# Attention, gated MLP and top-2 experts on one core: one addition becomes a tensor_reduce, and the conversion of the first weights is spread in another way

## The chip, the cores and the metric

The kernel runs on one NeuronCore of a Trainium2 chip. A NeuronCore has five engines that run side by side, each through its own list of instructions in order, and wait for each other by semaphores: TensorE (PE in the profile; the loading of weights into it is PEld), VectorE (DVE), ScalarE (ACT), GpSimd (POOL) and SyncE (SP), which here issues most of the DMAs. The metric is the device time of one execution in microseconds (us); lower is better.

## The reference

Three layers follow each other. All inputs come from the host in one launch.

```
# 1. attention: B=4, H=8 heads, S=576, D=64; heads 0-3 see the last 32 positions,
#    heads 4-7 every 32nd position before them
scores = where(mask, q @ k.T / sqrt(D), -1e9)
attn   = exp(scores - max(scores))
attn   = attn / (sum(attn) + 1e-9)
x      = attn @ v                         # 2304 tokens x 512
# 2. MLP: 512 -> 2048 -> 512
h = x @ w_in ;  x = (h * sigmoid(1.702 * h)) @ w_out
# 3. eight experts, two per token, chosen by noisy logits: 512 -> 1024 -> 512
out[t] = sum over the 2 experts of weight * (relu(x @ w1[e]) @ w2[e])
```

The weights w_in and w_out of the MLP arrive as 64-bit floats.

## The kernel before, in words

**Numbers in two halves.** TensorE multiplies rounded 32-bit values (fp32r). To keep the precision, a matrix is held as a high part (the rounded value) and a low part (what is left), and each product is three matmuls: high times high, high times low, low times high. L460, L461 and L462 are these three of the first MLP product, L486 to L488 those of the second. L462 is the first of the three that reads the low part of a weight.

**MLP weights.** The hidden 2048 columns are 16 slices of 128 (`fc`). Slice fc has two pieces of 512 columns: piece (fc, 0) belongs to w_in and is read by `m1_l1` (L451), piece (fc, 1) to w_out and is read by `m1_l2` (L478). A piece goes through four stations:

- `w_raw` (L355) loads its 64-bit words by DMA on SP's queue; there are four such buffers;
- `w_bits` (L416) makes 32-bit floats of them with three operations of 128x512 on DVE: L421, L424, L428. In the prologue the intermediate value stands in PSUM (`pb`), afterwards in SBUF (`cv`);
- `w_split` (L388) makes the high part on ACT (L392) and the low part on POOL (L393). It takes what was converted before the last call of `w_split`, so a piece is split one call later than the next one at hand;
- then `w_raw` asks for the piece two slices on.

`w_step` (L402) hands out one piece per call; the code takes one of the three operations at each `next(conv)`.

**Attention.** It is cut into groups (one batch, a pair of heads, a part of the positions). A group goes through scores on PE (L222 or L237), masking and minimum on DVE (L185), exponents and their sums on ACT (L190), `normalize` (L193), transposes on PE (L250 or L255), a copy on ACT, the product with v on PE (L267 or L277), and the high and low part of x (ACT L206, DVE L209). In `normalize` DVE adds 1e-9 to the sums (L194) and takes the reciprocal (L196); for the first 28 groups POOL multiplies by it (L198), afterwards DVE does (L202). The small numbers of a group stand in a tile `st` with four buffers.

**Order of the work.** Everything around the change is in an order written by hand: engines PE, ACT, DVE and POOL run their instructions in the order of the code.

- The prologue (loop at L901, steps k = 0, 1, ...) works through the first 14 groups of attention, so that the MLP can begin on the first tokens. In the steps named by `CONVAT` a piece of the weights is converted too. `warm` matmuls (L888) on a tile of ones keep PE busy.
- Then come the slices (loop at L957, number i). Slices 0 to 7 work on tokens 0 to 383 with fc = i; slices 8 to 23 work on tokens 384 to 767 with fc = i - 8, and so on. In slices 0 to 7 DVE, ACT and POOL also do two groups of attention each. A slice runs `m1_l1` of itself, some attention, `m1_l2` of the slice before, more attention. Each slice converts one piece in its first half (L968, `conv = w_step()`); the line `conv = w_step() if i < HALFC and not i % 2 or ...` adds a second one in its second half for i = 0, 2, 4, 6. `w_split` is called twice in a slice, in the middle and at the end.
- In the second half of a slice with a second piece, DVE does L421, L424, L194, L428 and L196 in this order, since `normalize` takes one operation of the piece between its own two.

## Time and profile before

| what | value |
|---|---|
| three runs | 971.8, 973.03 and 973.61 us, median 973.03 |
| the profiled execution | 971.91 us |
| its span in the trace | 970.1 us |
| PE busy | 951.4 us (98%) |
| DVE busy | 531.3 us (55%) |
| ACT busy | 387.0 us (40%) |
| POOL busy | 218.0 us (22%) |
| first matmul of the MLP (L460) | 35.25 us after the span's start |
| granted TensorE clock | mean 0.998 |

Busy time counts matmuls with a modelled end, so a busy PE is not a PE at its peak. The chain of work that ended last is PE for 82%, DVE for 8%. DVE's busy tenths are 7 to 9 of 10 in the first 120 us and 3 to 6 later. A duration in the trace contains the time that an instruction waited after it had begun, so the same operation on the same tile can show 0.15 and 1.26 us.

### The profile page before, as it was taken

The page shows a single profiled execution, that of the slowest core. Times are in us where ns is not written, and L with a number is a line of the kernel's source. Part 1 is how long each engine was busy: PE and PEld are TensorE (multiplying, and loading weights), DVE is VectorE, ACT ScalarE, POOL GpSimd, SP SyncE. Part 2 cuts the span into 40 slices and gives each one's busy share as a digit, 9 for nine tenths or more (in the row PEclk, how much of TensorE's full clock was granted, in tenths as well). Part 3 has the DMA queues.
Part 4 walks back from the last instruction along what each step waited for, and adds up shares of the span by engine and source line. Part 5 has one row for each costly group of instructions (what it writes and reads, how often), then busy time and mean ns, then how long its engine had stood idle before and what let it go on. Part 6 is the DMA issues. An engine that isn't in the chain of part 4 may idle for free.

```text
span 970.1 us, 15925 instructions
## 1 busy us (share of the span) xinstructions
PE 951.4 (98%) x5706; PEld 839.3 (87%) x5706; DVE 531.3 (55%) x1518; ACT 387.0 (40%) x1031; POOL 218.0 (22%) x206
## 2 busy tenths in 40 slices
PE   7999999999999999999999999999999999999996
PEld 4778899898888889899898998888988889898994
DVE  7899865467646745632666343545546363635511
ACT  6865533344444444223254242333424242433411
POOL 3566231020200100020230522050412305050303
PEclk9999999999999999999999999999999999999999
DMA  9754521052324236301064158275674938576503
GB/s 337 254 193 164 173 70 66 1 118 61 57 88 113 68 70 216 149 1 66 3 194 142 31 140 217 87 176 172 140 221 109 237 113 204 151 170 177 107 1 53
DMA packets 83793, 123.93 MB, mean 128 GB/s; under 512 B 13488, under 2 KB 42800, under 8 KB 83696
## 3 DMA queue, kind: packets, MB, share of 16 engines
q1 hardware_dynamic: 73888, 102.92, 34.5%
q0 software_dynamic: 9824, 19.98, 11.0%
q8 instruction: 45, 0.74, 0.3%
q14 instruction: 36, 0.29, 0.1%
HBM read 93.33 MB, written 29.68 MB: 127 GB/s over the span
## 4 chain that ended last, share of the span: by engine, by line
PE 82%; DVE 8%; issue 5%; ACT 2%; DMA 1%; POOL 1%; SPq 0%; POOLq 0%; DVEq 0%; ACTq 0%
PE pb L827 6%; PE pb L826 6%; PE pb L828 6%; PE pb L486 6%; PE pb L845 6%; PE pb L460 6%; PE pb L847 6%; PE pb L846 6%; PE pb L461 6%; PE pb L462 6%; PE pb L488 6%; PE pb L487 6%; DVE area L428 1%; PE pb L237 1%; PE pb L222 1%
## 5 line engine op out<-in xcount | busy, mean ns | idle before, releaser
L831 DVE SCALAR_TENSOR_TENSOR ht<-pb,ht 128x352 fp32r<-128x352 f32 (+2 forms) x126 | 59.2, 472 | 170.8 <-ACT ht L830 170.8
L460 PE MATMUL pb<-xt,w 128*128 128x384 f32 x384 | 131.8, 343 | 0.0
L461 PE MATMUL pb<-xt,w 128*128 128x384 f32 x384 | 129.6, 338 | 0.0
L462 PE MATMUL pb<-xt,w 128*128 128x384 f32 x384 | 129.5, 337 | 0.0
L830 ACT ACTIVATE ht<-pb 128x352 fp32r<-128x352 f32 (+2 forms) x126 | 53.1, 424 | 182.0 <-PE pb L828 181.2
L845 PE MATMUL pb<-w,ht 128*128 128x512 f32 (+1 forms) x315 | 124.0, 394 | 0.0
L846 PE MATMUL pb<-w,ht 128*128 128x512 f32 (+1 forms) x315 | 123.3, 391 | 0.0
L847 PE MATMUL pb<-w,ht 128*128 128x512 f32 (+1 forms) x315 | 123.2, 391 | 0.0
L863 POOL DMA_INDIRECT out<-y,el x40 | 63.1, 1578 | 266.5 <-ACT y L862 237.8
L486 PE MATMUL pb<-w,g 128*128 128x512 f32 x288 | 118.2, 410 | 0.3 <-ACT g L474 0.2
L488 PE MATMUL pb<-w,g 128*128 128x512 f32 x288 | 113.2, 393 | 0.0
L487 PE MATMUL pb<-w,g 128*128 128x512 f32 x288 | 112.5, 391 | 0.0
L469 DVE SCALAR_TENSOR_TENSOR th<-th,pb 128x384 f32<-128x384 f32 x96 | 52.7, 549 | 107.0 <-ACT th L465 107.0
L655 POOL DMA_INDIRECT lst<-pay,si x36 | 35.7, 992 | 326.9 <-DVE si L652 285.3
L680 DVE TENSOR_TENSOR w<-raw,w 128x512 fp32r<-128x512 f32 x128 | 85.3, 688 | 28.5 <-ACT w L679 27.5
L465 ACT ACTIVATE th<-pb 128x384 f32<-128x384 f32 x96 | 46.9, 489 | 128.4 <-PE pb L462 118.0
L679 ACT CAST w<-raw 128x512 fp32r<-128x512 f32 x128 | 76.0, 619 | 35.9 <-DMA raw<-wm 33.0
L826 PE MATMUL pb<-xt,w 128*128 128x352 f32 (+1 forms) x256 | 84.0, 328 | 0.0
L828 PE MATMUL pb<-xt,w 128*128 128x352 f32 (+1 forms) x256 | 83.5, 326 | 0.0
L827 PE MATMUL pb<-xt,w 128*128 128x352 f32 (+1 forms) x256 | 83.4, 326 | 0.0
L460 PEld LDWEIGHTS pb<-xt,w 128*128 128x128 f32 x384 | 72.1, 188 | 4.8 <-issue 1.0
L461 PEld LDWEIGHTS pb<-xt,w 128*128 128x128 f32 x384 | 72.1, 188 | 3.8 <-DVE xt L209 0.2
(193 smaller groups left out, 1925.1 us busy)
## 6 DMA issues: line engine op xcount, KB each, us to landing
raw<-wm SPq DMA_DIRECT2D x136, 256.0 KB, 3.0
area<-wm SPq DMA_DIRECT2D x28, 512.0 KB, 4.3
xs<-g SPq DMA_DIRECT2D x24, 256.0 KB, 3.7
out<-zero SPq DMA_DIRECT2D x7, 768.0 KB, 7.3
att<-attS SPq DMA_DIRECT2D x20, 253.0 KB, 4.5
qk<-attL SPq DMA_DIRECT2D x16, 304.0 KB, 4.3
tr<-xs SPq DMA_DIRECT2D x24, 176.0 KB, 3.4
att<-attL SPq DMA_DIRECT2D x8, 496.0 KB, 8.3
```

What stands on the lines that cost most here:

```text
L460: nc.tensor.matmul(ps, w[0][:, a], X[c][:, 0, kc, :], start=(n == 0), stop=False)
L461: nc.tensor.matmul(ps, w[0][:, a], X[c][:, 1, kc, :], start=False, stop=False)
L462: nc.tensor.matmul(ps, w[1][:, a], X[c][:, 0, kc, :], start=False, stop=(n == 3))
L486: nc.tensor.matmul(o, g[:, 0, a], w[0], start=((c, fc) in FIRST), stop=False)
L487: nc.tensor.matmul(o, g[:, 0, a], w[1], start=False, stop=False)
L488: m = nc.tensor.matmul(o, g[:, 1, a], w[0], start=False, stop=((c, fc) in LAST))
L826: nc.tensor.matmul(ps, w[:, 0, a], x[:, 0, kc, :], start=(kc == 0), stop=False)
L827: nc.tensor.matmul(ps, w[:, 0, a], x[:, 1, kc, :], start=False, stop=False)
L828: nc.tensor.matmul(ps, w[:, 1, a], x[:, 0, kc, :], start=False, stop=(kc == 3))
L845: nc.tensor.matmul(o, hi, w[:, 0, 512:], start=(fc == 0), stop=False)
L846: nc.tensor.matmul(o, hi, w[:, 1, 512:], start=False, stop=False)
L847: m = nc.tensor.matmul(o, lo, w[:, 0, 512:], start=False, stop=(fc == NF2 - 1))
```

## The change

The 1e-9 is no longer added in place. One tile `stats` takes the place of the four `st`; its row 2 holds 1e-9 for good, and a `tensor_reduce` sums rows 1 (the sums) and 2 into row 3, from which the reciprocal goes to row 4. In the prologue four pieces are converted and not six, in steps 5, 7, 9 and 11 and not in 4, 6, 7, 9, 11 and 13. Slices 1, 2, 4, 5, 9 and 10 convert two pieces, and not slices 0, 2, 4 and 6. The load of the sixth group of attention moves ahead of the first piece of weights.

```
-CONVAT = (4, 6, 7, 9, 11, 13)
+TWICE = (1, 2, 4, 5, 9, 10)
+CONVAT = (5, 7, 9, 11)
...
+    stats = const.tile([128, 4, 5, 4], F32, name="stats")
...
         def normalize(p, st, q, nt, w, pool, conv):
-            nc.vector.tensor_scalar(st[:q, 1, :nt], st[:q, 1, :nt], 1e-9, None, op0=OP.add)
+            nc.vector.tensor_reduce(st[:q, 3, :nt], st[:q, 1:3, :nt].rearrange("p a t -> p t a"),
+                                    axis=AX.X, op=OP.add)
             next(conv, None)
-            nc.vector.reciprocal(st[:q, 2, :nt], st[:q, 1, :nt])
+            nc.vector.reciprocal(st[:q, 4, :nt], st[:q, 3, :nt])
...
-            st = tmp.tile([128, 3, 4], F32, tag="st", name="st", bufs=4)
...
-                    self.sm[i] = g_scores(self.gs[i], self.ld[i], banks[i % len(banks)])
+                    self.sm[i] = g_scores(self.gs[i], self.ld[i], banks[i % len(banks)], stats[:, i % 4])
...
+        nc.vector.memset(stats[:, :, 2], 1e-9)
...
-        att.load(5)
+        att.load(6)
         w_raw(0, 0)
         att.load(2)
         w_raw(0, 1)
-        att.load(1)
         w_raw(1, 0)
         w_raw(1, 1)
...
-            conv = w_step() if i < HALFC and not i % 2 or i >= SMALLS else iter(())
+            conv = w_step() if i in TWICE or i >= SMALLS else iter(())
```

The line numbers of the changed kernel are 2 or 3 higher: L194 becomes L196, L196 becomes L199, L198 becomes L201, L393 becomes L395, L421, L424 and L428 become L423, L426 and L430, L460 to L462 become L462 to L464, L469 becomes L471, L476 becomes L478.

**DVE in the prologue, before**, from the first operation of piece (0, 1) to that of piece (1, 0) (`area_130` and `area_135` are their raw buffers):

```order
L421 TENSOR_SCALAR pb7_70<-area_130 128x512
L185 ISA att_128,st_240<-pb0_63,cs_74 126x126
L185 ISA st_240 126x1
L185 ISA att_128,st_240<-pb0_63,cs_74 126x126
L185 ISA st_240 126x1
L424 SCALAR_TENSOR_TENSOR pb7_70<-area_130,pb7_70 128x512
L428 SCALAR_TENSOR_TENSOR area_130<-area_130,pb7_70 128x512
L194 TENSOR_SCALAR st_214<-st_214 126x2
L196 RECIPROCAL st_214<-st_214 126x2
L209 TENSOR_TENSOR xt_101<-pb5_68,xt_101 128x7x18
L421 TENSOR_SCALAR pb7_70<-area_135 128x512
```

The same step with the change, up to the first operation of piece (0, 1), now `area_134`:

```order
L187 ISA att_130,stats_78<-pb0_63,cs_74 126x126
L187 ISA stats_78 126x1
L187 ISA att_130,stats_78<-pb0_63,cs_74 126x126
L187 ISA stats_78 126x1
L196 TENSOR_REDUCE stats_78<-stats_78 126x2
L199 RECIPROCAL stats_78<-stats_78 126x2
L212 TENSOR_TENSOR xt_102<-pb5_68,xt_102 128x7x18
L423 TENSOR_SCALAR pb7_70<-area_134 128x512
```

Two steps of the prologue (4 and 13) lose a conversion, and the one of step 6 moves to step 5.

**POOL in slices 3 to 5, before** (`w1_5_626` and `w1_6_713` are the slots of the weights of fc = 5 and 6; L476 is once in a slice, L198 twice):

```order
L198 TENSOR_TENSOR att_532<-att_532,st_780 72x2x72
L476 TENSOR_TENSOR g_806<-th_805,g_806 128x384
L393 TENSOR_TENSOR w1_5_626<-area_627,w1_5_626 128x512
L198 TENSOR_TENSOR att_620<-att_620,st_822 126x2x126
L393 TENSOR_TENSOR w1_5_626<-area_675,w1_5_626 128x512
L198 TENSOR_TENSOR att_622<-att_622,st_856 126x2x126
L476 TENSOR_TENSOR g_880<-th_879,g_880 128x384
L198 TENSOR_TENSOR att_707<-att_707,st_896 126x2x126
L393 TENSOR_TENSOR w1_6_713<-area_714,w1_6_713 128x512
```

The same engine with the change, from slice 4 to slice 6 (`w1_5_715`, `w1_6_793`, `w1_7_896` are the slots of fc = 5, 6, 7):

```order
L201 TENSOR_TENSOR att_584<-att_584,stats_78 126x2x126
L478 TENSOR_TENSOR g_840<-th_839,g_840 128x384
L201 TENSOR_TENSOR att_667<-att_667,stats_78 126x2x126
L395 TENSOR_TENSOR w1_5_715<-area_716,w1_5_715 128x512
L201 TENSOR_TENSOR att_669<-att_669,stats_78 126x2x126
L478 TENSOR_TENSOR g_914<-th_913,g_914 128x384
L395 TENSOR_TENSOR w1_5_715<-area_751,w1_5_715 128x512
L201 TENSOR_TENSOR att_747<-att_747,stats_78 72x2x72
L395 TENSOR_TENSOR w1_6_793<-area_794,w1_6_793 128x512
L478 TENSOR_TENSOR g_986<-th_985,g_986 128x384
L395 TENSOR_TENSOR w1_6_793<-area_823,w1_6_793 128x512
L395 TENSOR_TENSOR w1_7_896<-area_897,w1_7_896 128x512
```

Before, the place behind the second L198 of slice 4 is that of piece (6, 0); now it is that of piece (5, 0). The split of piece (fc, 0) for fc = 5, 6, 7 has moved from one slice earlier to the end of the slice just ahead of the one that reads it.

**PE at the start of slice 5, before**:

```order
L277 MATMUL pb7_70<-att_620 64x126
L255 MATMUL pb6_69<-cs_74,att_622 126x126 [waits Pool_49]
L255 MATMUL pb6_69<-cs_74,att_622 126x126
L237 MATMUL pb5_68<-att_709 126x126 [waits DMAHW2_49,DVE_49]
L237 MATMUL pb5_68<-att_709 126x126
L460 MATMUL pb1_64<-xt_101,w1_5_626 128x384
L461 MATMUL pb1_64<-xt_101,w1_5_626 128x384
L462 MATMUL pb1_64<-xt_101,w1_5_626 128x384
```

With the change:

```order
L279 MATMUL pb7_70<-att_582 64x126
L257 MATMUL pb6_69<-cs_74,att_584 126x126 [waits Pool_49]
L257 MATMUL pb6_69<-cs_74,att_584 126x126
L239 MATMUL pb5_68<-att_669 126x126 [waits DMAHW7_49,DVE_49]
L239 MATMUL pb5_68<-att_669 126x126
L462 MATMUL pb1_64<-xt_102,w1_5_715 128x384 [waits Activation_49]
L463 MATMUL pb1_64<-xt_102,w1_5_715 128x384
L464 MATMUL pb1_64<-xt_102,w1_5_715 128x384 [waits Pool_49]
```

The first matmul of the slice now waits for ACT (the high part) and the third for POOL (the low part). The same two waits stand at the start of slices 3, 4, 6 and 7 with the change, and at none of them before.

## Rows read from the trace of the kernel before

**Rows 1.** Busy us (and instructions) by stretch: PE, PEld, DVE, ACT, POOL, clock, DMA share.
```profile
0.00:35.20 35.20, 28.82 (x217) 18.72 (x218) 27.10 (x143) 25.65 (x107) 16.13 (x25) 1.00 0.94 350
35.20:86.20 51.00, 48.98 (x340) 39.73 (x339) 45.87 (x131) 31.85 (x110) 31.78 (x31) 1.00 0.49 164
```

**Rows 2.** Waits of PE from 35.2 to 90 us: total us, times, longest.
```profile
PE pb L277 <- DVE xt L209: 1.0, 2, 0.5
PE pb L267 <- DVE xt L209: 0.5, 1, 0.5
PE pb L277 <- DVE st L185: 0.4, 1, 0.4
```

**Rows 3.** DVE in the prologue, in order of time: start us, duration us, instruction.
```profile
10.16 0.69 DVE L421 TENSOR_SCALAR pb<-area 128x512 int32<-128x512 int32 x1 [0.69 <-DMA area<-wm]
...
20.54 0.70 DVE L421 TENSOR_SCALAR pb<-area 128x512 int32<-128x512 int32 x1
...
24.78 0.69 DVE L421 TENSOR_SCALAR pb<-area 128x512 int32<-128x512 int32 x1
...
31.77 0.26 DVE L185 CUSTOM_DVE_ANT_0 att<-pb,cs 128x96 f32<-128x96 f32 x1
...
34.34 0.25 DVE L185 CUSTOM_DVE_ANT_0 att<-pb,cs 128x96 f32<-128x96 f32 x1
```

**Rows 4.** PE in slices 3 to 7, the third and last L462 of each.
```profile
57.88 0.34 PE L462 MATMUL pb<-xt,w 128*128 128x384 f32 x1
...
63.33 0.34 PE L462 MATMUL pb<-xt,w 128*128 128x384 f32 x1
...
64.91 0.33 PE L462 MATMUL pb<-xt,w 128*128 128x384 f32 x1
...
69.88 0.34 PE L462 MATMUL pb<-xt,w 128*128 128x384 f32 x1
...
71.47 0.34 PE L462 MATMUL pb<-xt,w 128*128 128x384 f32 x1
...
76.44 0.34 PE L462 MATMUL pb<-xt,w 128*128 128x384 f32 x1
...
78.03 0.34 PE L462 MATMUL pb<-xt,w 128*128 128x384 f32 x1
...
82.45 0.34 PE L462 MATMUL pb<-xt,w 128*128 128x384 f32 x1
```

**Rows 5.** DVE in slices 3 to 6.
```profile
60.54 0.53 DVE L469 SCALAR_TENSOR_TENSOR th<-th,pb 128x384 f32<-128x384 f32 x1
...
63.30 1.26 DVE L194 TENSOR_SCALAR st<-st 126x2 f32<-126x2 f32 x1
...
67.09 0.53 DVE L469 SCALAR_TENSOR_TENSOR th<-th,pb 128x384 f32<-128x384 f32 x1
...
69.92 0.43 DVE L421 TENSOR_SCALAR cv<-area 128x512 int32<-128x512 int32 x1
...
71.72 0.16 DVE L196 RECIPROCAL st<-st 126x2 f32<-126x2 f32 x1
...
78.98 0.56 DVE L469 SCALAR_TENSOR_TENSOR th<-th,pb 128x384 f32<-128x384 f32 x1
```

**Rows 6.** POOL in slices 3 and 4.
```profile
62.79 1.74 POOL L393 TENSOR_TENSOR w<-area,w 128x512 fp32r<-128x512 f32 x1
...
72.59 1.47 POOL L393 TENSOR_TENSOR w<-area,w 128x512 fp32r<-128x512 f32 x1
```

**Rows 7.** ACT at the end of slice 6.
```profile
82.55 0.62 ACT L392 CAST w<-area 128x512 fp32r<-128x512 f32 x1
```

**Rows 8.** All of L194: duration in ns, minimum, median, maximum.
```profile
L194 DVE TENSOR_SCALAR st<-st x64: 151/169/1257, 7.2 to 387.2; 126x2 f32<-126x2 f32 x32, 128x3 f32<-128x3 f32 x24, 72x2 f32<-72x2 f32 x8
```

**Rows 9.** The nearest tensor_reduce: busy us, mean ns of one.
```profile
L651 DVE TENSOR_REDUCE sc<-sm 128x3 f32<-128x24 f32 x12 | 2.1, 176 | 0.3
```

**Rows 10.** Columns as in rows 1, after the last matmul.
```profile
961.00:962.00 1.00, 0.00 (x0) 0.00 (x0) 0.00 (x0) 0.65 (x1) 0.08 (x1) 1.00 0.80 68
...
965.00:966.00 1.00, 0.00 (x0) 0.00 (x0) 0.00 (x0) 0.00 (x0) 0.00 (x0) 0.86 0.41 72
```

## The prediction

> **What bounds the kernel now.** I began with the busy time by stretch. In the first 35.2 us PE is busy for 28.8 and DVE for 27.1 us; from 35.2 to 86.2 us, the slices 0 to 7, PE is busy for 49.0 of 51.0 us and DVE for 45.9 [rows 1]. The reader is to see two stages with different limits. In the prologue PE is partly busy with matmuls on ones that nobody needs, so its length is set by the chain through DVE. In slices 0 to 7 PE does needed work almost without a gap, with DVE close behind. After that PE is the bound and has nothing before it that this change touches: what happens up to about 110 us moves the whole rest of the program, and the end with it, by the same amount. So the question is by how much the start of the MLP moves, and how long PE waits in slices 0 to 10.

> Second, the waits of PE in the slices: 1.0, 0.5 and 0.4 us, 1.9 in all [rows 2]. All are on DVE. None is on a weight. The third view is the order of time: DVE in the prologue [rows 3], PE's first and second half matmuls of a slice [rows 4], and DVE, POOL and ACT in slices 3 to 6 [rows 5 to 7], because the order of the changed kernel has new waits for weights there.

> **The change part by part.**

> *Two conversions fewer in the prologue.* From the first operation of one piece to that of the next but one step later DVE takes 24.78 - 20.54 = 4.24 us; two steps without a conversion take 34.34 - 31.77 = 2.57 us [rows 3]. A conversion costs 1.67 us in its step. Its three operations of 0.69 us are 2.07 us, the most it can be where DVE never idles. Two fewer: 3.3 us, at most 4.1. The first piece is now loaded behind one more group and the constants, but is also wanted one step later; DVE waited 0.69 us for it before [rows 3] and may wait as long again, so I leave that at nothing, with 0.7 either way. At the end four steps without conversion stand together, and there the step is limited by the round trip through PE, DVE and ACT and not by DVE's work; I take 0.4 us off. Gain 2.9 us, between 2.0 and 4.5.

> *tensor_reduce for the addition.* L194 takes 151 ns at best and 1257 ns at worst [rows 8]. The long ones end with a POOL operation: the one at 63.30 lasts until 64.56 [rows 5], and POOL's L393 that began at 62.79 ends at 64.53 [rows 6]. So the addition waits for POOL, up to 1.1 us at a time. A tensor_reduce on a larger input takes 176 ns [rows 9], so without a wait the new operation costs nothing that counts. Whether it waits beside POOL no row shows. Between no wait and the same wait I take no wait, since the reciprocal right behind it, also from SBUF to SBUF, takes 0.16 us in the same slices (at 71.72) [rows 5].

> [...]

> What it is worth for PE: DVE gains up to 1.1 us at an addition, twice in a slice. That takes away the three kinds of waits in rows 2, as does the single conversion in slice 0. Gain 1.9 us, between 1.0 and 1.9.

> *Pieces converted later.* This is the term that decides. Four pieces and not six are ready at the first slice. With one piece in slices 0, 3, 6, 7 and two in 1, 2, 4, 5, piece (fc, 0) of slices 3 and 4 gets its low part in the middle of the slice before, that of slices 5, 6 and 7 at the very end of the slice before. I write s for the start of the last L462 of a slice; the low part is first read by the third L462 of the next.

> Slice 4 to 5. PE needs the low part at 69.88 - 64.91, at s + 4.97 [rows 4]. The split at the end of slice 4 stands on POOL behind the second normalize, which waits for DVE's reciprocal, which comes after all three operations of the second piece. The same list of instructions ran before in the same slice: from L469 at 67.09 [rows 5] to the end of L393 at 72.59 + 1.47 = 74.06 [rows 6], 6.97 us, with no long L194 in it. L469 can begin 0.95 us after s at the earliest (78.98 against 78.03) [rows 4, 5]. The low part is there at s + 7.92: PE waits 2.95 us. At the pace of before it would be 74.06 - 69.88 = 4.2, which is the upper bound; if the DVE operation that meets L476 did not wait for it, 2.5.

> Slice 5 to 6. PE needs it at 76.44 - 71.47 = 4.97, less the 0.5 that PE waited in that slice (one of the two of 1.0 in rows 2), so s + 4.47. The chain is the one above, but POOL now also splits (5, 1) in mid-slice. In slice 3 such a split ends 64.53 - 60.54 = 3.99 us after L469 [rows 5, 6], and the second piece's L421, which came 69.92 - 67.09 = 2.83 after it, would meet it and wait up to 1.16. So s + 7.92 to 9.08, a wait of 3.45 to 4.6; I take 4.0, the middle.

> Slice 6 to 7. One piece, no normalize. PE needs it at 82.45 - 78.03, less the other 0.5, at s + 3.92. ACT's L392 at the end of that slice began at 82.55 [rows 7], s + 4.02 without the 0.5; plus 0.62 and 1.47 for L392 and L393: s + 6.11. A wait of 2.2; 1.5 to 2.9, if the chain is 0.7 shorter or longer.

> Slice 3 to 4. Needed at 63.33 - 57.88, less 0.4 of wait, at s + 5.05; there at s + 0.95 + 3.99 = s + 4.94 plus whatever DVE is late. DVE's slice 3 took 67.09 - 60.54 = 6.55 with one conversion; slice 2 will have two (+1.67) and a split in mid-slice (+1.16) and no long addition (-1.1): 8.3 against PE's 64.91 - 57.88 - 0.4 = 6.6. It can be 0 to 1.9 late; I take 0.9. Slice 2 to 3 has the same arithmetic with DVE not late: nothing.

> New waits: 0.9 + 2.95 + 4.0 + 2.2 = 10.0 us, from 7.5 to 13.5.

> *Two pieces in slices 9 and 10.* About 1.7 us more of DVE each. The cover is PE's own work while DVE, which had time to catch up during the new waits, starts slice 8 without being late. If that cover is gone, up to 3 us.

> *Sum.* -2.9 - 1.9 + 10.0 = +5.2 us. Against the profiled execution's own 971.91 us (span 970.1) that is 977.1; against the median of the three runs, 973.03, it is 978.2. I say 978.0. From the lower bound (7.5 - 4.5 - 1.9 = +1.1) to the upper (13.5 + 3 - 2.0 - 1.0 = +13.5): 973 to 986.

> **The rivals.**

> *Faster: the splits come in time.* Place: the end of slices 4, 5 and 6. If the chain from L471 to the end of the split shrank from 6.97 to 4.0 us, PE would find each low part ready and keep both gains: 973.0 - 4.8 = 968.2. For it: DVE and POOL no longer hold each other up at the addition. Against it: the 6.97 has no long addition in it, and what is in line is the same as before. It decides at 4.0 us, where PE needs the low part less the 0.95; I see how the chain could lose half a microsecond, not three.

> *A wash: half of it.* The waits come out at 5 us, because in each slice the wait before lets DVE and POOL start fresh and the splits in mid-slice do not collide. Then gains and waits cancel: 973.2. For it: every wait of PE is time for DVE. Against it: my terms already start DVE with no lateness.

> *The clock falls.* PE idles for 3 and 4 us. After the last matmul the granted clock stays at 1.00 and is 0.86 in the stretch 965 to 966, so it fell to the lower level about 4.8 us after the work stopped [rows 10]. The waits stay below that, though the third is near. [...]

> *The reduce waits as the addition did.* Then the change does not do what it says; DVE stays late by about 1.2 us in slices 1 to 4 and the term of slice 4 goes to its upper end, with the old waits kept: 978.0 + 1 + 1 = 980.

> **How the numbers follow.** The forecast 0.63 (975 to 982 alone), the wash 0.13, the faster rival 0.07, the clock 0.10, the waiting reduce 0.07. A difference of 0.2% (1.9 us) is about what a measurement of this kernel can tell from no change. Faster by more than that takes the faster rival: 0.07. Within it the wash and the low end of the forecast: 0.13. Slower: 0.80. The range that holds 8 in 10 leaves out the faster rival and the far upper end: 973 to 984.

> **What would show it.** The first matmul of the MLP near 32.3 us and not 35.25; no addition (now L196) above 0.3 us; waits of PE on POOL's L395 before the third matmul of slices 5, 6, 7 of about 3, 4 and 2 us, and a smaller one in slice 4; no waits of PE on DVE's xt before that; from slice 8 on nothing but a shift. If PE shows no waits on weights there, the whole term of 10 us is wrong, and the time will be below 970.

## The result, and the profile after

The changed kernel takes 986.77 us, median of 6 runs (985.87 to 989.18); the kernel before takes 972.68 us, median of 6 (971.8 to 975.5). The ratio is 1.0144, with a 95% interval from 1.0132 to 1.0155. I forecast 978.0 and a range up to 984: the direction was right, the size was not. It is 14.1 us slower and not 5.2.

The profiled execution took 986.96 us with a span of 985.2. Ahead of all else stands the busy time by stretch, cut at the start of the MLP, at slice 2, in the middle of slice 7 and in the middle of slice 14 (columns as in [rows 1]; the last number is GB/s of the DMAs):

```profile
0.00:33.73 33.73, 28.38 (x217) 18.47 (x217) 23.09 (x138) 25.08 (x107) 14.24 (x23) 0.95 0.93 344
33.73:47.40 13.67, 13.67 (x128) 11.16 (x126) 10.08 (x38) 10.33 (x38) 6.06 (x7) 1.00 0.48 168
47.40:95.22 47.82, 38.76 (x207) 29.72 (x205) 29.93 (x93) 22.56 (x72) 25.62 (x24) 0.89 0.39 130
95.22:133.88 38.66, 36.36 (x232) 31.55 (x231) 34.75 (x88) 19.77 (x56) 13.55 (x10) 1.00 0.53 178
```

In the third stretch PE is idle for 47.82 - 38.76 = 9.1 us, and the granted clock, 1.00 all through this stage before, has a mean of 0.89. The prologue has a mean of 0.95 where it had 1.00. In the fourth PE is idle for another 2.3 us. Beside [rows 2], where PE waited only for DVE, stand the waits after, from 34 to 95 us and from 94 to 135 us:

```profile
PE pb L464 <- POOL w L395: 6.5, 5, 2.8
PE pb L462 <- ACT w L394: 2.3, 3, 1.0
PE pb L279 <- DVE stats L187: 0.2, 1, 0.2
...
PE pb L490 <- DVE g L478: 1.1, 2, 0.7
PE pb L252 <- ACT pt L253: 0.9, 1, 0.9
PE pb L489 <- POOL w L395: 0.3, 1, 0.3
```

PE's third and last L464 of slices 3 to 7, which answer to [rows 4] (L462 there):

```profile
56.41 0.34 PE L464 MATMUL pb<-xt,w 128*128 128x384 f32 x1
...
62.21 0.44 PE L464 MATMUL pb<-xt,w 128*128 128x384 f32 x1 [0.51 <-POOL w L395]
...
63.88 0.33 PE L464 MATMUL pb<-xt,w 128*128 128x384 f32 x1
...
71.81 0.44 PE L464 MATMUL pb<-xt,w 128*128 128x384 f32 x1 [2.11 <-POOL w L395]
...
74.46 0.52 PE L464 MATMUL pb<-xt,w 128*128 128x384 f32 x1
...
83.60 0.69 PE L464 MATMUL pb<-xt,w 128*128 128x384 f32 x1 [2.85 <-POOL w L395]
...
86.65 0.52 PE L464 MATMUL pb<-xt,w 128*128 128x384 f32 x1
...
93.38 0.44 PE L464 MATMUL pb<-xt,w 128*128 128x384 f32 x1 [0.73 <-POOL w L395]
```

The numbers in brackets are less than what was lost, since an L462 or L463 runs alone in front of each wait. What counts is the time between rows: from the last L464 of slice 4 to the third of slice 5 it is 71.81 - 63.88 = 7.93 us. The forecast had s + 7.92. The last L464 of slices 5 and 6 takes 0.52 us where others take 0.33: there the granted clock is at a lower level, 0.50 of the full one where it fills a whole stretch:

```profile
70.00:72.00 2.00, 0.18 (x1) 0.19 (x2) 0.96 (x7) 0.88 (x4) 2.00 (x3) 1.00 0.16 58
72.00:74.00 2.00, 2.00 (x8) 2.00 (x9) 0.00 (x0) 0.00 (x0) 0.33 (x1) 0.58 0.46 143
74.00:76.00 2.00, 2.00 (x12) 1.24 (x11) 0.40 (x1) 0.84 (x2) 0.00 (x0) 0.57 0.29 119
...
82.00:84.00 2.00, 0.40 (x1) 0.40 (x2) 0.04 (x1) 0.00 (x0) 1.54 (x2) 0.64 0.28 113
84.00:86.00 2.00, 2.00 (x7) 2.00 (x7) 0.00 (x0) 0.00 (x0) 0.00 (x0) 0.50 0.63 205
86.00:88.00 2.00, 2.00 (x11) 1.24 (x10) 0.21 (x1) 0.66 (x2) 0.00 (x0) 0.50 0.14 57
88.00:90.00 2.00, 2.00 (x8) 1.62 (x7) 1.97 (x4) 1.42 (x4) 1.03 (x1) 0.65 0.00 0
```

It fell to that level while PE stood waiting (slice 6: 0.50 from 83.0 to 83.6 us) or just after (slice 5: 1.00 until 72.2, 0.54 from there to 73.5 us). By the shares above PE then worked at half speed for an estimated 3.4 us behind the third L464 of slice 5 and 5.8 us from that of slice 6 on.

The sum's row, for [rows 8]: minimum, median and maximum of 64 are close together.

```profile
L196 DVE TENSOR_REDUCE stats<-stats x64: 141/158/164, 7.0 to 401.2; 126x2 f32<-126x4 f32 x32, 128x3 f32<-128x6 f32 x24, 72x2 f32<-72x4 f32 x8
```

The next table is the measure for all that follows: by how many us the first l1 matmul of a slice starts later than in the trace of before (worked out from PE's order of time; the first column has the time itself).

| kernel | MLP starts | 0 | 3 | 8 | 14 | 26 |
|---|---|---|---|---|---|---|
| before | 35.25 | 0 | 0 | 0 | 0 | 0 |
| after | 33.73 | -1.52 | -2.11 | +11.04 | +13.99 | +14.02 |
| e1_reduce | 35.77 | +0.52 | +0.49 | -1.47 | -1.46 | -1.44 |
| e2_schedule | 33.26 | -1.99 | -2.62 | +13.02 | +15.99 | +16.02 |
| e3_early | 34.17 | -1.08 | -0.09 | +1.71 | +1.72 | +1.75 |
| e4_keepbusy | 34.07 | -1.18 | -1.77 | +8.52 | +11.48 | +11.51 |
| e5_later | 33.73 | -1.52 | -2.10 | +12.06 | +11.77 | +16.85 |
| e6_ahead | 34.11 | -1.14 | -0.14 | +1.91 | +1.44 | +2.15 |
| e7_fill | 35.31 | +0.06 | +0.08 | -1.89 | -1.90 | -1.87 |
| e8_loads | 33.49 | -1.76 | -2.31 | +9.23 | +13.23 | +13.74 |
| e9_none | 33.91 | -1.34 | -1.97 | +12.19 | +11.88 | +16.34 |
| e10_actnorm | 34.10 | -1.15 | -1.69 | +11.66 | +13.63 | +13.63 |
| e11_moreact | 35.05 | -0.20 | -0.72 | +12.16 | +15.13 | +15.16 |
| e12_moreact_old | 36.64 | +1.39 | +1.41 | -0.55 | -0.55 | -0.52 |
| e13_five | 38.33 | +3.08 | +3.06 | +3.33 | +3.32 | +3.34 |
| e14_actnorm_old | 35.47 | +0.22 | +0.25 | -1.71 | -0.83 | -0.81 |

Behind slice 26 these shifts stay within about 1 us until slice 95; in the experts' part another -0.5 to +4 us came in, which no edit here touches. In this trace it is a transfer: ACT's cast at 618.53 waited 5.5 us for an expert's weights, 4.2 in the trace of before, and PE's L828 then waits 1.4 us once. So the table says where time went up to slice 26, and the medians say how much in all.

### The profile page after: what moved, and what is told of

It reads as the page before. It is cut to its first block, busy times and chain, and to the rows that moved or that the text cites. A ratio compares the mean times of both kernels' runs of the same rounds, so it can differ in the third digit from the quotient of the medians.

```text
span 985.2 us, 15956 instructions
## 1 busy us (share of the span) xinstructions
PE 957.3 (97%) x5704; PEld 842.0 (85%) x5704; DVE 524.2 (53%) x1519; ACT 388.6 (39%) x1031; POOL 216.7 (22%) x206
## 3 DMA queue, kind: packets, MB, share of 16 engines
q1 hardware_dynamic: 73888, 102.92, 34.7%
## 5 line engine op out<-in xcount | busy, mean ns | idle before, releaser
L464 PE MATMUL pb<-xt,w 128*128 128x384 f32 x384 | 131.5, 342 | 6.5 <-POOL w L395 6.5
L462 PE MATMUL pb<-xt,w 128*128 128x384 f32 x384 | 132.9, 346 | 2.3 <-ACT w L394 2.3
L463 PE MATMUL pb<-xt,w 128*128 128x384 f32 x384 | 130.9, 341 | 0.0
L471 DVE SCALAR_TENSOR_TENSOR th<-th,pb 128x384 f32<-128x384 f32 x96 | 52.9, 551 | 123.4 <-ACT th L467 123.4
L682 DVE TENSOR_TENSOR w<-raw,w 128x512 fp32r<-128x512 f32 x128 | 85.6, 690 | 33.0 <-ACT w L681 31.7
L828 PE MATMUL pb<-xt,w 128*128 128x352 f32 (+1 forms) x256 | 84.1, 329 | 0.0
L464 PEld LDWEIGHTS pb<-xt,w 128*128 128x128 f32 x384 | 73.0, 190 | 8.1 <-POOL w L395 8.1
L462 PEld LDWEIGHTS pb<-xt,w 128*128 128x128 f32 x384 | 72.9, 190 | 7.7 <-ACT w L394 2.9
```

Of the source, the lines that this page charges most:

```text
L462: nc.tensor.matmul(ps, w[0][:, a], X[c][:, 0, kc, :], start=(n == 0), stop=False)
L463: nc.tensor.matmul(ps, w[0][:, a], X[c][:, 1, kc, :], start=False, stop=False)
L464: nc.tensor.matmul(ps, w[1][:, a], X[c][:, 0, kc, :], start=False, stop=(n == 3))
L682: nc.vector.tensor_sub(w[:, 1, o], raw, w[:, 0, o].bitcast(F32))
L828: nc.tensor.matmul(ps, w[:, 0, a], x[:, 0, kc, :], start=(kc == 0), stop=False)
```

## The experiments

**The sum alone, and the places alone.** In e1_reduce `CONVAT`, `TWICE` and the loads are those of before:

```
-TWICE = (1, 2, 4, 5, 9, 10)
-CONVAT = (5, 7, 9, 11)
+TWICE = (0, 2, 4, 6)
+CONVAT = (4, 6, 7, 9, 11, 13)
```

> The kernel before with the new sum alone (the memset constant and tensor_reduce); six pieces in the prologue, slices 0, 2, 4 and 6 convert two. Theory: the reduce only takes away VectorE's waits at that sum (the longest was 1257 ns, the middle one 169 ns), and PE feels little of it: 970.7 to 972.7 us against 972.7 before. Rival: the reduce itself brings part of the loss of the changed kernel: above 975 us.

Measured: 970.25 us (969.24 to 971.31), ratio 0.9971 (0.9957 to 0.9984). e2_schedule is the other half, the old `tensor_scalar` with the new places:

> The kernel before with the old sum (tensor_scalar) and the new places of the conversions: four pieces in the prologue, two in slices 1, 2, 4, 5, 9 and 10. Theory: the whole loss is in the places of the conversions: 985 to 989 us, PE waits for POOL's low part in slices 3 to 7 as in the changed kernel. Rival: sum and places each bring a part: 978 to 983 us.

Measured: 989.16 us, ratio 1.0165 (1.0142 to 1.0188). The sum is worth 2.5 us with the old places and 989.16 - 986.77 = 2.4 with the new ones. So the places of the conversions cost 16.4 us, and the new sum takes 2.4 of them back (e2_schedule has four runs, 987.72 to 991.85; in the traces the stretch from slice 0 to slice 8 says the same, 15.01 us lost for 12.56). In e1_reduce PE is busy for all of the 40 us from 50 to 90: the old waits of [rows 2] are gone, as the table's fall from +0.49 to -1.47 says.

**Are the pieces late, or are they too many?** e3_early converts four in the prologue, the other two in slices 1 and 3; e6_ahead adds a second piece to slice 0 and has one late one, in slice 12, and not two:

```
-TWICE = (1, 2, 4, 5, 9, 10)
+TWICE = (0, 1, 2, 3, 4, 6)      (e3_early)
+TWICE = (0, 1, 2, 4, 5, 12)     (e6_ahead)
```

> The changed kernel with the same four pieces in the prologue, but the two that are left convert in slices 1 and 3 (two conversions in slices 0, 1, 2, 3, 4 and 6), so that every weight of an l1 is split at least a slice ahead. Theory (late weights): the shift of 13.2 us over slices 3 to 7 and that of 2.9 us over slices 9 to 11 both go; 1.5 us of the prologue stays won, and VectorE, busy 9.3 to 9.6 of 10 us there, gives back up to 3.6 us in slices 0 to 3: 970 to 975 us, no waits for L395. Rival (the work itself: two conversions more beside PE cost wherever they stand): above 978 us.

> The changed kernel with a second conversion in slice 0, so that every later piece is converted one place earlier ((5,0) in slice 3 and not in slice 4, (6,0) in slice 4, (7,0) in slice 5), and one second conversion less behind (slice 12 alone instead of 9 and 10). Theory (it is the lateness of these pieces by one place, not their number in slices 1 to 5): no PE wait for a weight in slices 4 to 7, VectorE's waits of 1 to 3 us in slices 1 to 5 instead, 971 to 974.5 us. Rival (the number: ten conversions in slices 1 to 5 hold PE up wherever each stands): over 979 us.

Measured: 973.8 us, ratio 1.001 (1.0000 to 1.0019), and 974.66 us, ratio 1.0019 (1.0009 to 1.0028). In e6_ahead the conversions of slices 1 to 5 are the same in number as in the changed kernel; each works on the piece that comes next. That alone takes the shift at slice 8 from +11.04 to +1.91. So most of the loss is lateness by one place. Against the expectation, not all of it went: the low parts of slices 6 and 7 still come late in e6_ahead, and its shift rises by 2.0 us from slice 6 to slice 8.

```profile
77.20 0.44 PE L464 MATMUL pb<-xt,w 128*128 128x384 f32 x1 [0.65 <-POOL w L395]
...
84.26 0.44 PE L464 MATMUL pb<-xt,w 128*128 128x384 f32 x1 [1.07 <-POOL w L395]
```

What PE waits for in e3_early:

```profile
PE pb L279 <- DVE xt L212: 3.0, 3, 1.1
...
PE pb L279 <- DVE stats L187: 1.3, 1, 1.3
```

These are the waits of [rows 2], grown: with two conversions more, DVE is late. From slice 0 to slice 8 e3_early loses 2.79 us where e1_reduce wins 1.99, 4.8 us for two conversions.

**The clock.** e4_keepbusy puts matmuls that nothing reads where PE waited:

```
+BUSY = {5: (2, 9), 6: (4, 13), 7: (3, 3)}
...
+                fillers = BUSY.get(fc, (0, 0)) if c == 0 and n == 0 else (0, 0)
+                for _ in range(fillers[0]):
+                    warm(PB[(fc + 1) % 2])
                 nc.tensor.matmul(ps, w[0][:, a], X[c][:, 0, kc, :], start=(n == 0), stop=False)
                 nc.tensor.matmul(ps, w[0][:, a], X[c][:, 1, kc, :], start=False, stop=False)
+                for _ in range(fillers[1]):
+                    warm(PB[(fc + 1) % 2])
```

> The changed kernel with matmuls on ones, that nothing reads, ahead of the first and of the third matmul of l1 in slices 5 (2 and 9), 6 (4 and 13) and 7 (3 and 3), where PE waited; they go to the other bank of l1. Theory (the fall of the clock is a second price of the wait, and comes from PE's idle time): the granted clock stays 1.00 from 70 to 90 us, the waits for L395 keep their place, and the 3.1 us at half speed come back: 983 to 984.5 us. Rival (the clock falls for another reason): the clock falls there all the same, 986 to 988 us.

Measured: 982.42 us, ratio 1.0101 (1.0081 to 1.0121). The busy time by stretch:

```profile
70.00:80.00 10.00, 9.73 (x54) 6.03 (x53) 6.45 (x20) 4.98 (x16) 5.42 (x5) 1.00 0.22 76
80.00:90.00 10.00, 9.25 (x49) 5.41 (x47) 5.47 (x10) 2.83 (x7) 5.38 (x5) 1.00 0.28 100
```

The clock stays at 1.00. At slice 8 the shift is 11.04 - 8.52 = 2.5 us smaller; as it was 0.34 us larger at slice 3 (-1.77 for -2.11), the fillers win 2.9 us between the two. Of these, 0.96 and 1.39 us lie within the matmuls of l1 in slices 5 and 6. Another 0.22 and 0.31 lie behind them: from the last L464 (here L470) of a slice to the third of the next it takes 8.92 us for 9.14 and 6.42 for 6.73. The waits themselves stay: without the fall of the clock the weights are still late. The medians differ by 4.35, more than expected; of the profiled executions 1.9 us of the difference lie in the experts' part, where no filler stands, so I take 2.9 for the clock. Why the medians show more is not explained.

**The two conversions of slices 9 and 10.** The second piece of a slice and the first of the next are split in one call. So the two second conversions make two pairs of low parts (x2 in POOL's rows). Here is DVE, and then POOL, of the changed kernel in order of time where these pairs stand, while PE is at slices 11 and 12:

```profile
116.08 2.53 DVE L205 TENSOR_SCALAR pl<-pl,stats 128x96 f32<-128x96 f32 x3
...
122.65 2.72 DVE L205 TENSOR_SCALAR pl<-pl,stats 128x96 f32<-128x96 f32 x3
```

```profile
115.27 3.09 POOL L395 TENSOR_TENSOR w<-area,w 128x512 fp32r<-128x512 f32 x2 [4.54 <-ACT w L394]
...
122.71 2.60 POOL L395 TENSOR_TENSOR w<-area,w 128x512 fp32r<-128x512 f32 x2 [4.35 <-ACT w L394]
```

DVE's three multiplications, 0.63 us by themselves (103.28 in this trace), last here until POOL's pairs are through (118.61 and 125.37 us, beside 118.36 and 125.31). e5_later moves the two conversions to slices 12 and 13, e9_none leaves them out until the pieces come behind slice 17, and e10_actnorm takes L205 off DVE:

```
-TWICE = (1, 2, 4, 5, 9, 10)
+TWICE = (1, 2, 4, 5, 12, 13)    (e5_later)
+TWICE = (1, 2, 4, 5)            (e9_none)

-                nc.vector.tensor_scalar(p[:q, t, :w], p[:q, t, :w], st[:q, 4, t:t + 1], None, op0=OP.mult)
+                nc.scalar.mul(p[:q, t, :w], p[:q, t, :w], st[:q, 4, t:t + 1])    (e10_actnorm)
```

> The changed kernel with the two conversions of slices 9 and 10 in slices 12 and 13 instead, where VectorE is busy 6.7 of 10 us; slices 0 to 8 as in the changed kernel. Theory (the second conversion in slices 9 and 10 makes VectorE later than PE there): the shift of 2.9 us between the starts of slices 8 and 14 goes and nothing comes in its place: 983.4 to 984.6 us. Rival (it only moves): a wait of the same size in slices 12 to 15, 986 to 988 us.

> The changed kernel without the second conversions of slices 9 and 10 (two in slices 1, 2, 4 and 5 alone); the last two full pieces then follow behind slice 17. Theory (from slice 9 on VectorE has no room for a second conversion, wherever it stands up to slice 15): the starts of slices 8 to 17 keep the shift that slice 8 has, 2.5 to 3 us of the changed kernel's loss go, 983 to 985 us. Rival (pieces that come later make a wait behind slice 17): the shift comes back there, 986 us or more.

> The changed kernel with the three multiplications of a pair's weights by the reciprocal on ScalarE and not VectorE (line 205; in slices 9 and 10 the three took 2.53 and 2.72 us of VectorE beside two low parts on POOL, 0.63 without). Theory (VectorE is the late one in slices 9 and 10, by what it waits there for POOL): the shift between the starts of slices 8 and 14 falls from 2.95 to under 1 us, 983.5 to 985.5 us. Rival (ACT's casts or POOL's low parts set the pace there): the shift stays at 2 to 3 us, 986 to 988 us.

Measured: 988.8 us, ratio 1.0162 (1.0147 to 1.0178); 988.93 us, 1.0162 (1.0145 to 1.0179); 984.69 us, 1.0123 (1.0098 to 1.0149). In e5_later and e9_none the shift indeed stands still between slices 8 and 14, so the second conversions did cost the 2.95 us there. But nothing is saved. Both are 1.0 to 1.2 us later than the changed kernel at slice 8; in both the clock fell in slice 7 too, with 2.64 and 2.60 us for its matmuls of l1 and not 1.67. e5_later then pays 5.1 us in slices 15 and 16, where PE waits for the g of ACT (0.8 us) and of DVE (2.1) and the clock falls once more (0.64 from 140 to 144 us). In e9_none weights are late for their slices again, this time behind slice 21:

```profile
162.04 0.50 PE L488 MATMUL pb<-w,g 128*128 128x512 f32 x1 [0.85 <-ACT g L476]
169.77 0.44 PE L462 MATMUL pb<-xt,w 128*128 128x384 f32 x1 [1.09 <-ACT w L394]
170.66 0.44 PE L464 MATMUL pb<-xt,w 128*128 128x384 f32 x1 [0.26 <-POOL w L395]
177.22 0.51 PE L488 MATMUL pb<-w,g 128*128 128x512 f32 x1 [0.38 <-ACT w L394]
```

The rivals were right in both (e5_later lost more than its rival said). In e10_actnorm the median lies where the theory had it, but the step between slices 8 and 14 is still 1.97 us, nearer to the rival's 2 to 3 than to the theory's 1, and its four runs lie far apart (983.56 to 987.88). So moving L205 won some 1 us of the 2.95 in the trace, and no more can be said. The blocking moved to the next operations of DVE:

```profile
117.21 1.61 DVE L430 SCALAR_TENSOR_TENSOR area<-area,cv 128x512 int32<-128x512 int32 x1
118.85 1.51 DVE L423 TENSOR_SCALAR cv<-area 128x512 int32<-128x512 int32 x1
```

Alone they take 0.69 and 0.42 us. Two low parts close behind each other cost DVE some 2 us, here as there (2.53 and 2.72 less 0.63 each), and also in e5_later, where a pair at 130.13 us made L478 take 1.64 and L423 1.51 us, alone 0.55 and 0.42. The second pair of e10_actnorm met no DVE operation. How much of the 2.95 us is this blocking and how much the 1.8 us of work that each conversion adds to DVE, no run separates.

**The prologue.** Nine traces with four pieces have the MLP start at 33.26 to 34.17 us, mean 33.84; four with six pieces at 35.25 to 35.77, mean 35.45. The gain is 1.6 us, 0.8 for a piece. Why not 2.9? From before to after DVE's work in the prologue fell by 27.10 - 23.09 = 4.0 us, but its idle time rose from 8.1 to 10.6: the steps then waited for something else. The lower clock of the changed kernel's prologue (0.50 from 17.7 to 21.1 us) is not it: e3_early has 1.00 there and starts at 34.17. Five runs asked further. e8_loads puts back the old order of the loads:

> The changed kernel with the old order of the loads (five pieces of attention, a weight, two, a weight, one, two weights) and still four pieces converted in the prologue. Theory (with two conversions gone PE and ACT set the prologue's last 8 us, ACT is busy 4.00 of 4 us from 24 to 32): the order of the loads matters little, the first matmul of the MLP between 33.3 and 34.2 us as in the three traces with the new order, 986 to 988 us. Rival (the weights that land 1.2 us later took the gain): the MLP starts at 32.3 to 32.8 us, 984.8 to 986 us.

Measured: 986.69 us, ratio 1.014 (1.0125 to 1.0156), start at 33.49: the order of the loads is not it. e7_fill asks for the clock, in e1_reduce:

```
+            for _ in range(7 if k == 9 else 0):
+                warm(PB[att.na % 3])
```

> The kernel with the new sum and the old places (e1_reduce, 970.25 us) with seven more matmuls on ones in the prologue, in the 1.63 us that PE waits for VectorE ahead of 20.38 us; behind that wait the clock stood at 0.57 from 20 to 24 us. Theory (the wait's price is mostly the clock): the clock stays 1.00 from 20 to 24 us, the first matmul of the MLP comes 0.5 to 1.5 us earlier than 35.77, 968.7 to 969.8 us. Rival (the prologue ends when VectorE does, whatever PE's clock): the clock stays up and the MLP starts at 35.5 to 36 all the same, 970 to 970.7 us.

Measured: 970.82 us, ratio 0.9978 (0.9969 to 0.9987). From 20 to 24 us, e1_reduce and then e7_fill:

```profile
20.00:24.00 4.00, 3.62 (x17) 2.26 (x18) 3.76 (x20) 2.75 (x12) 3.75 (x5) 0.57 1.03 412
```

```profile
20.00:24.00 4.00, 4.00 (x33) 2.56 (x31) 3.76 (x20) 3.68 (x16) 3.38 (x5) 1.00 1.03 408
```

The clock stayed up, the MLP started 0.46 us earlier, within the scatter of the six-piece traces, and the time is no better than 970.25. Half speed (0.57) cost little here, where PE has room. e11_moreact and e12_moreact_old add four copies on ACT near the prologue's end, to the changed kernel and to e1_reduce:

```
+            if 10 < k < 15:
+                nc.scalar.copy(tmp.tile([128, CH], F32, tag="th", name="more", bufs=1), cs[:, :CH])
```

> The changed kernel with four more copies of 128x384 on ScalarE, which nothing reads, in the prologue's steps 11 to 14 (some 0.4 to 0.5 us each, 1.6 to 2 us together). Theory (with four conversions the prologue's end is set by ACT, busy 7.50 of 7.50 us from 26 to 33.5): the first matmul of the MLP comes later by all of it, at 35.0 to 36.0 us against 33.3 to 34.2. Rival (VectorE still sets it): by under 0.6 us.

> The same four copies on ScalarE in the kernel with the new sum and the old places (e1_reduce), where six pieces are converted and VectorE is busy 7.0 to 7.7 of each 7.5 to 8 us. Theory (there VectorE sets the prologue's end and ACT has room): the first matmul of the MLP at 35.4 to 36.6 us against 35.77, under half of the 1.6 to 2 us added. Rival (ACT sets it in both): 37.2 us or more.

Measured, one run each: 989.45 and 972.66 us, starts at 35.05 and 36.64. The copies took 513 and 496 ns at the median, so 2.05 and 1.98 us were added. Against the means above the start moved by 1.21 and by 1.19 us. Both starts lie on the edge of what the theories said, and the two kernels do not differ: ACT seems to be in the chain with either number of pieces, by some 0.6 of its work. These are single traces, the starts without the copies scatter by 0.9 and 0.5 us, and in e12_moreact_old the clock was at its lower level from 28.3 to 31.7 us (the matmuls of L891 took 0.61 and 0.63 us there, 0.38 elsewhere), so this is an indication and not more. e13_five has five pieces:

```
-TWICE = (0, 2, 4, 6)
-CONVAT = (4, 6, 7, 9, 11, 13)
+TWICE = (0, 2, 3, 4, 6)
+CONVAT = (4, 6, 7, 9, 11)
```

> The kernel with the new sum and the old places, with five pieces converted in the prologue and a second conversion in slice 3 for the sixth (two in slices 0, 2, 3, 4 and 6). Theory (past the first piece removed the prologue is set by ACT's and PE's steps, so the gain is not 1.67 us for each piece but ends near 1.7 us for both): the first matmul of the MLP at 33.8 to 34.4 us; slice 3 gives it back, 970.5 to 972.5 us. Rival (a gain of one size for each piece, some 0.9 us): 34.7 to 35.1 us.

Measured: 972.49 us, ratio 0.9994 (0.9985 to 1.0003). The median is at the upper end of the theory's range. The profiled execution was the slowest of ten, 975.14, and its start, 38.33, is outside both theories. It can't say where the MLP usually starts: a weight came late (DVE's L423 waited 0.82 us for its transfer at 25.77), PE waited 1.35 us, and the end of the prologue ran at a lower clock (mean 0.73 from 26 to 33.5 us).

```profile
28.98 0.38 PE L891 MATMUL pb<-ones 128*128 128x512 bf16 x1 [1.35 <-DVE xt L212]
...
30.23 1.44 PE L224 MATMUL pb<-att 128*128 128x96 f32 x6
```

Six L224 take 0.81 us where the clock is 1.00 (at 24.98 in the same trace). What a piece is worth in the prologue stays a measured 0.8 us without a proved cause.

**A faster kernel.** e14_actnorm_old tries L205 on ACT in e1_reduce:

> The kernel with the new sum and the old places (e1_reduce), with the three multiplications by the reciprocal on ScalarE as in e10_actnorm. Theory (no PE wait in slices 8 to 12 comes from VectorE there, so relief buys nothing): 969.8 to 970.7 us. Rival (the 0.8 us that e10_actnorm won behind slice 30, beside its 1 us in slices 9 and 10, is to be had here too): 968.5 to 969.5 us.

Measured: 970.69 us, ratio 0.9975 (0.9966 to 0.9984), the same as e1_reduce. In e1_reduce PE waits for DVE 0.2 us in all from 48 to 135 us, so there was next to nothing to win; with the multiplications on ACT it waits once for ACT, in slice 9:

```profile
93.46 0.50 PE L488 MATMUL pb<-w,g 128*128 128x512 f32 x1 [1.14 <-ACT part L450]
```

e1_reduce, the new sum with the old places, beats both kernels, and nothing here is measurably faster than it.

## Why the prediction was wrong

The late weights and their waits came as forecast. What failed are two terms that the sum put at nothing: the clock (2.9 us) and the two conversions in slices 9 and 10 (2.95 us); and the gain in the prologue, taken at 2.9 us, was 1.5. The measured time lies above even the sum of all upper ends, 986, which had no place for the clock.

*Right: the new waits and their mechanism.* The rows named for it came in the places named. From the last L464 of a slice to the third of the next, against the same span before, slices 3 to 4 lost 0.35 us (forecast: 0.9 less an old wait of 0.4), 4 to 5 lost 2.96 (2.95), 5 to 6 lost 4.17 (4.0 - 0.5 = 3.5), 6 to 7 lost 2.31 (2.2 - 0.5 = 1.7). In slice 4 the chain from L471 to the end of L395 took 71.77 - 64.83 = 6.94 us, for 6.97 in the forecast, and the collision foreseen in mid-slice 5 is there: L423 at 78.54 took 1.37 us, to 79.91, beside POOL's L395 of 77.92, done at 79.63.

```profile
64.83 0.55 DVE L471 SCALAR_TENSOR_TENSOR th<-th,pb 128x384 f32<-128x384 f32 x1 [1.74 <-ACT th L467]
...
78.54 1.37 DVE L423 TENSOR_SCALAR cv<-area 128x512 int32<-128x512 int32 x1
```

```profile
70.32 1.45 POOL L395 TENSOR_TENSOR w<-area,w 128x512 fp32r<-128x512 f32 x1
...
77.92 1.71 POOL L395 TENSOR_TENSOR w<-area,w 128x512 fp32r<-128x512 f32 x1
```

*Right: the reduce does not wait.* 141 to 164 ns, also beside a low part on POOL (0.15 us at 60.94, within POOL's L395 of 60.43 to 62.15), and 2.4 to 2.5 us won where I had 1.9. The tensor_scalar took up to 1257 ns before [rows 8] and 1228 in e2_schedule, the reduce at most 164 ns after and 165 in e1_reduce. Nor is it the slower of the two: the medians are 169 ns for the tensor_scalar and 158 and 157 for the reduce.

*Wrong: "The waits stay below that."* This dismissed the rival with the clock, at a chance of 0.10. I had taken one fall, some 4.8 us after the last matmul [rows 10], for the time that a wait may last; that trace has 1.00 up to 965.7 us and 0.50 behind:

```profile
966.00:967.00 1.00, 0.00 (x0) 0.00 (x0) 0.00 (x0) 0.00 (x0) 0.00 (x0) 0.50 0.00 0
```

In the trace after, the clock fell at waits recorded as 2.11 and 2.85 us. Inside slices 5 and 6 PE lost 1.06 and 1.46 us, and e4_keepbusy gives 2.9 back in all: there matmuls with no use filled the waits and the clock stayed at 1.00.

*Wrong in size: slices 5 to 6 and 6 to 7.* The two spans above that came out 0.6 to 0.7 us too long lie behind the stretches at the lower clock, but with the clock at 1.00 e4_keepbusy still has 8.92 and 6.42 us there, for 8.47 and 6.12 in the forecast. So 0.2 and 0.3 us are the clock and 0.45 and 0.3 the terms themselves. In slice 5 the collision cost L423 1.37 - 0.43 = 0.94 us, where I had taken the middle of 0 and 1.16.

Of the other rivals none came: the chain did not shrink (6.94 us), so neither the faster kernel nor the wash, and the reduce did not wait.

*Wrong: the cover in slices 9 and 10.* Two conversions were to be hidden by PE's own work. They cost 2.95 us, what the text gave as the price "if that cover is gone". I had counted 1.7 us of DVE for each, and not the 2 us more that a pair of low parts in a row takes from DVE; that the cover failed is shown by e5_later and e9_none, that the pair is why is in part argued.

*Wrong in size: the prologue,* 1.5 us in this trace and 1.6 on average for 2.9.

*Wrong by 0.6 us: slice 3,* forecast to start without a wait; its third L464 waited 0.35 for POOL.

Together: 5.2 as forecast, +1.4 for the prologue, +2.5 for the clock inside slices 5 and 6, +1.3 behind them (0.5 of it the clock), +0.6 in slice 3, +2.95 in slices 9 and 10 make 13.95; the table has +14.02 and the medians 14.1. That they agree so well is in part luck, as the experts' part moved the profiled executions by -0.5 to +4 us.

## What to carry to other kernels

## What the runs showed of the hardware that I had not expected

The length of a wait alone did not say whether the clock would fall. In slice 5 of e8_loads PE waited as long as in the changed kernel, at the same place, and the clock stayed at 1.00 behind it (it fell in slice 6):

```profile
71.34 0.44 PE L464 MATMUL pb<-xt,w 128*128 128x384 f32 x1 [2.11 <-POOL w L395]
...
72.00:74.00 2.00, 2.00 (x16) 1.58 (x15) 0.04 (x1) 0.56 (x2) 0.00 (x0) 1.00 0.67 205
```

In e1_reduce a wait of 1.63 us in the prologue was followed by 0.57; in e2_schedule one of 1.66 us was followed by 1.00 throughout:

```profile
17.14 0.70 PE L238 MATMUL pb<-att 128*126 128x126 f32 x4 [1.66 <-DMA att<-attS]
```

```profile
16.00:20.00 4.00, 2.85 (x24) 1.90 (x25) 3.90 (x20) 2.56 (x13) 2.48 (x3) 1.00 1.04 416
20.00:24.00 4.00, 4.00 (x35) 2.91 (x34) 3.90 (x16) 3.63 (x16) 2.31 (x3) 1.00 1.03 414
```

And POOL held up more of DVE than the tensor_scalar of L194 [rows 8]. L430, a scalar_tensor_tensor with both inputs in SBUF, takes 0.68 to 0.69 us alone and 1.08 to 1.67 where it starts beside a POOL instruction (9 of 22 in e1_reduce: eight beside L478, one beside a low part). In the prologue, where one of its inputs is in PSUM, it takes 0.69 us also beside a low part (four times, in the trace of before at 15.64, 22.17, 26.64 and 30.71, there L428). L471, also with one input in PSUM, takes 0.51 to 0.56 in either case.
